# Bounds from sums of squares, a bfloat16 spread and another start of an attention and two-MLP kernel

## The chip, the core and the metric

The kernel runs on one core of a Trainium2 chip. The metric is the device time of one execution in microseconds (us); the time of a kernel is the median of its runs. The engines are TensorE (PE, with its weight loads as PEld), VectorE (DVE), ScalarE (ACT), GpSimd (POOL) and SyncE (SP), which issues the DMAs. Each engine works through its own queue in order, and waits at the head of it.

## The reference

An attention with a memory is followed by two MLPs over the same 2304 tokens:

```python
scores = where(causal, -1e9, (q @ k.T) / 8)        # B, H, S, D = 4, 8, 576, 64
a = exp(scores - max); a /= sum(a) + 1e-9
q_p = phi(q)                                       # elu(q) + 1
mem_out = (q_p @ M_prev) / (q_p . z_prev + 1e-6)
g = 1 / (1 + exp(-beta))                           # beta: one number a head
x = g * mem_out + (1 - g) * (a @ v)                # -> 2304 x 512

h = x @ w_in                                       # 512 -> 2048, first MLP
x = softplus(h) @ w_out                            # 2048 -> 512

h = x @ w2_in                                      # second MLP
P = a0 + a1*h + a2*h^2 + a3*h^3
Q = 1 + |b0|*|h| + |b1|*h^2
out = (P / (Q + 1e-6)) @ w2_out
```

The weights arrive as 8-byte floats (8 MB a matrix), and the kernel makes 4-byte floats of them by shifts and masks.

## The kernel before, in words

**Passes and blocks.** Attention goes in seven passes (`PASSES`) over parts of the four batch entries, each of two or four units of heads. Passes 0 to 2 (`FA32 = 3`) work in float32. From pass 3 on, every matrix is split into a high and a low float16 part, and a product is three float16 matmuls. After each pass the first MLP runs over its tokens in blocks (`g1`: `w_in` and softplus; `g2`: `w_out`); block 0 is in float32 (`NF32 = 1`), the others in split float16. The second MLP takes all tokens in six blocks of 384 at the end (`x2load`, `h1`, `h2_`).

**Bounds.** A split needs a power of two that keeps the numbers in float16's range, so it needs an upper bound of the operand. The kernel takes a bound for each partition, and `pmax` makes it one for all partitions: GpSimd reduces it across partitions to a number in partition 0, and a float32 matmul with a row of ones (`one`) spreads it to all 128 partitions of a PSUM bank. For the weights and for q, k and v the bound of a partition is the root of a sum of squares, from an ACT Square with its accumulator (`half_bits` halves the exponent, `ROOT` mends it). For the attention output x (`xmx`, `xgroup`), for `M_prev` (`batch_scale`) and for the second MLP's input (`x2load`) it is the largest absolute value, from a DVE `tensor_reduce`.

**What sets the order.** Nearly every instruction is recorded by one helper (so nearly all rows carry L458) and put in order by a list scheduler (`Program.order`). It walks through simulated time with its own cost for each operation, its own idea of when a DMA lands, and a key for each operation (lower goes first). An operation that may run on several engines (`flex`) goes where the model ends it sooner. For PE the scheduler looks at work only `SLACK` ns after it thinks the data is ready, as long as there is other work. The engines' queues come out of this and are fixed. Keys: `EARLY` says which inputs are loaded between the pieces of `w_in`, `KEY_W1I` and `KEY_ST` place the conversion of weight pieces, the latter that of the second MLP's, which is done during the attention (`w2_early`, tile `a`).

**Filler matmuls.** `WARM` (256 columns, tile `mask` into bank 0) and `FILL` (64 columns, `mask` into bank 7) matmuls have the lowest priority on PE and stand wherever the scheduler's model has PE idle at the start, until they are used up.

**The softplus table.** ACT has three stages of function tables (`TABLES`). The load of the second, with softplus, comes after every Exp, Ln, Abs or Sign of the first stage; `consts()` has an Exp of `beta` (tile `gg`) and an Abs of the second MLP's `b` (tile `bb`). The exponentials of the attention are softplus too.

```python
def pmax(src, n, bk=None):
    m = tn("pmx", 8, 6)[0:1, 0:n]
    G.tensor_reduce(out=m, in_=src, axis=AX.C, op=ALU.max)
    ...
    PE.matmul(out=r, lhsT=one[0:1].to_broadcast([1, 128]), rhs=m, start=True, stop=True)
```

Of the kernel before, what the change touches and what calls it, by code (L numbers as in the profile page):

```python
# [9 lines left out]
F32 = mybir.dt.float32  # L10
# [14 lines left out]
LAG = 3  # L25
SLACK = 300.0
NLOW = 1
POOL_OPS = (ALU.add, ALU.subtract, ALU.mult, ALU.max, ALU.min)

QLATE = 80  # L30
KWIN = 100.0
LMIN = 300.0
EARLY = lambda load, u, consts, batch: (
    (lambda: load(u[0], 0, 1), lambda: load(u[1], 0, 1)),
    (lambda: load(u[0], 2), batch),
    (consts,),
    (lambda: load(u[1], 2),),
)
KEY_B0 = 40
KEY_S2 = 80  # L40
KEY_W1I = 50
KEY_P = (0, 0, 0, 0)
KEY_W1O = 25
KEY_LO = -20
SL_LO = 0.5
KEY_L = -20
KEY_U2 = -30
NF32 = 1
WR0 = 6
WARM = 120  # L50
KEY_SQ = 0.0
FILL = 400
FA32 = 3
B32 = (0, 1, 2, 3, 4, 5, 6)
PEC = 2.0
# [3 lines left out]
EARLY2 = {3: (0, 16)}  # L59
KEY_ST = 160  # L60
BACKLOG = 6000.0
# [79 lines left out]
def cost(eng, name, kw):  # L141
# [5 lines left out]
    if eng == "PE":  # L147
        if name == "transpose":
            return n / 1.2 + PEC
        f32 = kw["rhs"].dtype == F32  # L150
        if n <= 8:
            return 310
        if span(out)[1] == 64:
            return 107 if f32 else 27
        return n / (0.6 if f32 else 2.4) + PEC
# [27 lines left out]
class Program:  # L183
# [151 lines left out]
    def order(self):  # L335
# [38 lines left out]
        while len(done) < len(self.ops):  # L374
# [113 lines left out]
def attn_moe_moe2(ctx, tc, q, k, v, m_prev, z_prev, beta, w1i, w1o, w2i, w2o, ca, cb, out):  # L488
# [160 lines left out]

    one = const.tile([128, 1], F32, name="one")  # L650
    off = tn("off", 1, 1)
    pcnt = [0]

    def pmax(src, n, bk=None):
        m = tn("pmx", 8, 6)[0:1, 0:n]
        G.tensor_reduce(out=m, in_=src, axis=AX.C, op=ALU.max)
        if bk is None:

            pcnt[0] += 1
            bk = bank[7][:, 320 + pcnt[0] % 24 * 8:]  # L660
# [23 lines left out]
    def consts():  # L684
        P.bulk = True
        SP.dma_start(out=gg, in_=beta.partition_broadcast(128))
        SP.dma_start(out=aa, in_=ca.partition_broadcast(128))
        SP.dma_start(out=bb, in_=cb.partition_broadcast(128))
        P.bulk = False
        A.activation(out=gg, in_=gg, func=AF.Exp, scale=-1.0)  # L690
        ts(gg, gg, 1.0, None, ALU.add)
        V.reciprocal(gg, gg)
        ts(iog, gg, -1.0, 1.0, ALU.mult, ALU.add)
        ts(iog, iog, 2.0 ** -100, None, ALU.max)
        V.reciprocal(iog, iog)
        ts(iog15, iog, 2.0 ** -15, None, ALU.mult)
        A.activation(out=bb, in_=bb, func=AF.Abs)

    def consts2():
# [12 lines left out]
        ts(fr, r, 0.5, None, ALU.mult)  # L712
# [55 lines left out]
    def batch_scale(m):  # L768
# [405 lines left out]
    def attentions32(p):  # L1174
# [8 lines left out]
        if p.i >= NF32:  # L1183
            for h in (0, 2):
                V.tensor_reduce(out=xmx[:, p.i % 3, h:h + 2], in_=p.x[:, h:h + 2], axis=AX.X, op=ALU.max, apply_absolute_value=True)

# [3 lines left out]
    def xgroup(p):  # L1190
# [4 lines left out]
        bm = tn("xm")  # L1195
        V.tensor_reduce(out=bm, in_=xmx[:, p.i % 3], axis=AX.X, op=ALU.max)
        bx, s = pow2(pmax(bm, 1), 1, "xs")
        for c in range(4):
# [133 lines left out]
    def attention(u):  # L1332
# [5 lines left out]
        if u.nh == 4:  # L1338
# [5 lines left out]
            if u.p.i >= NF32:  # L1344
                V.tensor_reduce(out=xmx[:, u.p.i % 3, h // 2:h // 2 + 2], in_=u.p.x[:, h // 2:h // 2 + 2], axis=AX.X, op=ALU.max, apply_absolute_value=True)
        else:
# [9 lines left out]
            for q0, n, c in AVC[u.i % 2][0]:  # L1356
                av_out(u, 0, q0 + 256 - u.p.q0, n, c)
            V.tensor_reduce(out=xmx[:, u.p.i % 3, h // 2:h // 2 + 1], in_=u.p.x[:, h // 2], axis=AX.X, op=ALU.max, apply_absolute_value=True)

# [96 lines left out]

    P.key = -180
    for o in RAW:
        G.memset(vw(o, (10, D), F32)[64:128], 0.0)

    P.key = -150
    w1_load(0, 0)
    P.add("POOL", "memset", lambda out: make_identity(nc, out), {"out": idf})
# [5 lines left out]
    P.pkey = 1e6  # L1469
    for _ in range(WARM):  # L1470
        PE.matmul(out=bank[0][:, 0:256], lhsT=mask[:, 0:128], rhs=mask[:, 0:256], start=True, stop=True)
    for _ in range(FILL):
        PE.matmul(out=bank[7][:, 256:320], lhsT=mask[:, 0:128], rhs=mask[:, 0:64], start=True, stop=True)
    early = EARLY(load, units, consts, lambda: batch_load(passes[0]))
    for pc in range(16):
        P.key = -149 + pc
        if pc:
            w1_load(0, pc)
        P.key += 0.5
        for step in early[pc] if pc < len(early) else ():  # L1480
            step()
        P.key = KEY_W1I + pc * 0.1
        w1_bits(0, pc)
# [8 lines left out]
    group32(passes[0])  # L1492
    P.key = -90
    batch(passes[1])
# [44 lines left out]
    for which in range(2):  # L1539
# [12 lines left out]
        if which == 0:  # L1552
# [31 lines left out]
    def x2load(j):  # L1584
# [163 lines left out]
```

## Time and profile before

| | before |
|---|---|
| median of 3 runs | 982.77 us (981.68 to 983.07) |
| the profiled execution | 979.67 us, of it 977.8 us from the first to the last instruction |
| PE, DVE, ACT, POOL busy | 946.6, 876.3, 773.9, 240.6 us |
| DMA share of the span | 51.8% of 16 engines |

The span is the time from the first to the last instruction of the profiled execution; 1.9 us of its own time lie around it. Busy times are unions of an engine's instructions. The filler matmuls count as busy PE, so PE's share of the span tells little of the first 50 us. Float32 matmuls other than transposes stand in the trace as two records each.

### The profile page before, as it was taken

To read this page: it belongs to the slowest core of one execution; us is meant where nothing else is said; L and a number is where in the kernel's file an instruction comes from. 1 tells how busy PE (TensorE), PEld (TensorE's weight loads), DVE (VectorE), ACT (ScalarE), POOL (GpSimd) and SP (SyncE) were. 2 spreads that over 40 slices of the span, in tenths; PEclk is the share of its full clock that TensorE was granted. 3 is DMA by queue.
4 is the path that set the end of the run, shared out by engine and by line. 5 is a ranking of instruction groups with operands and counts; after the bars stand their busy time and mean duration, and the time that the engine had idled before them with its cause. 6 is when DMAs were issued, how large, how long until landed. Compare 5 with 4: busy or idle time off the path is not lost. (4 is left out here: it accounts for less than half of the span.)

```text
span 977.8 us, 23547 instructions
## 1 busy us (share of the span) xinstructions
PE 946.6 (97%) x8786; PEld 693.1 (71%) x8786; DVE 876.3 (90%) x2213; ACT 773.9 (79%) x1759; POOL 240.6 (25%) x437
## 2 busy tenths in 40 slices
PE   7999999999899999899899999999999999999998
PEld 6867787878688888788799997555555555555554
DVE  4999899998988997889779979999999999989995
ACT  4997988887887886886656858878788788887885
POOL 2454342221211232122103202112304123041111
PEclk9999999999999999999999999999999999999999
DMA  9998268777999898999997420001001000000000
GB/s 235 301 260 210 66 123 172 151 137 162 166 176 182 161 166 162 173 197 254 240 299 257 162 94 2 14 1 36 32 1 65 1 34 33 1 34 1 33 1 33
DMA packets 247587, 117.94 MB, mean 121 GB/s; under 512 B 218928, under 2 KB 225072, under 8 KB 247472
## 3 DMA queue, kind: packets, MB, share of 16 engines
q1 hardware_dynamic: 247472, 116.44, 51.8%
q8 instruction: 69, 1.13, 0.5%
q14 instruction: 46, 0.38, 0.1%
HBM read 63.45 MB, written 13.63 MB: 79 GB/s over the span
## 5 line engine op out<-in xcount | busy, mean ns | idle before, releaser
L458 PE MATMUL bank<-arena,w 128*128 128x160 f16 (+3 forms) x4448 | 411.0, 251 | 4.2 <-DVE arena L458 2.8
L458 PE MATMUL bank<-arena 128*128 128x384 f16 (+9 forms) x2820 | 341.4, 293 | 13.1 <-DVE arena L458 5.9
L458 PEld LDWEIGHTS <-w 128*128 128x128 f16 x4224 | 329.7, 98 | 28.4 <-issue 8.6
L458 ACT ACTIVATE arena<-bank,tiny 128x384 f32<-128x384 f32 (+8 forms) x512 | 275.1, 585 | 44.6 <-PE bank L458 36.0
L458 PEld LDWEIGHTS <-arena 128*128 128x128 f16 (+1 forms) x2464 | 164.9, 104 | 113.6 <-issue 23.4
L458 PE MATMUL bank<-arena,gr 128*128 128x512 f16 x864 | 201.2, 379 | 0.0
L458 PEld LDWEIGHTS <-gr 128*128 128x128 f16 x864 | 84.2, 98 | 91.9
L458 POOL TENSOR_SCALAR tiny<-tiny 128x1 f32<-128x1 f32 (+6 forms) x208 | 71.3, 344 | 285.7 <-DVE tiny L458 225.4
L458 ACT ACTIVATE bank<-bank,tiny 128x512 f32<-128x512 f32 (+4 forms) x200 | 106.7, 540 | 39.6 <-PE bank L458 15.5
L458 POOL TENSOR_TENSOR arena<-arena 128x384 f32<-128x384 f32 (+5 forms) x58 | 67.2, 1160 | 231.4 <-ACT arena L458 195.8
L458 DVE SCALAR_TENSOR_TENSOR arena<-bank,tiny,arena 128x512 f16<-128x512 f32 (+5 forms) x200 | 114.0, 594 | 7.5 <-ACT arena L458 6.5
L458 ACT ACTIVATE arena<-arena,tiny 128x128 f32<-128x128 f32 (+10 forms) x164 | 98.1, 624 | 11.5 <-DVE tiny L458 5.8
L458 ACT ACTIVATE lt<-arena,qe 128x384 f32<-128x384 f32 x96 | 59.1, 615 | 33.8 <-POOL arena L458 19.8
L458 DVE SCALAR_TENSOR_TENSOR arena<-arena,tiny 128x384 f16<-128x384 f32 (+5 forms) x112 | 79.1, 729 | 4.5 <-ACT arena L458 3.3
L458 DVE CUSTOM_DVE_ANT_0 bank<-bank,mask,tiny 128x384 f32<-128x384 f32 (+4 forms) x112 | 66.8, 609 | 3.2 <-PE bank L458 2.8
L458 DVE SCALAR_TENSOR_TENSOR bank<-bank,tiny,lt 128x384 f32<-128x384 f32 x96 | 59.4, 619 | 10.9 <-ACT lt L458 10.1
L458 DVE SCALAR_TENSOR_TENSOR arena<-arena,qe,lt 128x384 f32<-128x384 f32 x96 | 66.0, 687 | 2.8 <-ACT lt L458 2.8
L458 DVE SCALAR_TENSOR_TENSOR bank<-arena,tiny,bank 128x384 f32<-128x384 f32 x96 | 59.1, 616 | 1.2
L458 ACT ACTIVATE arena<-arena 128x640 f32<-128x640 f32 (+4 forms) x75 | 46.9, 626 | 16.1 <-DVE arena L458 9.3
L458 DVE TENSOR_TENSOR arena<-arena 128x384 f32<-128x384 f32 (+5 forms) x107 | 56.7, 534 | 1.7 <-ACT arena L458 1.4
L458 DVE TENSOR_SCALAR tiny<-tiny 128x1 uint32<-128x1 uint32 (+8 forms) x306 | 49.1, 180 | 9.4 <-ACT bank L458 4.8
L458 ACT ACTIVATE gr<-arena 128x384 f16<-128x384 f32 x86 | 44.7, 520 | 10.8 <-DVE arena L458 9.6
(121 smaller groups left out, 975.0 us busy)
## 6 DMA issues: line engine op xcount, KB each, us to landing
arena<-in_moe_w_out_dram SPq DMA_DIRECT2D x32, 512.0 KB, 5.5
arena<-in_moe_w_in_dram SPq DMA_DIRECT2D x24, 512.0 KB, 5.4
arena<-in_k_dram SPq DMA_DIRECT2D x44, 128.0 KB, 3.3
arena<-in_v_dram SPq DMA_DIRECT2D x44, 128.0 KB, 3.0
arena<-arena SPq DMA_DIRECT2D x32, 160.0 KB, 2.9
arena<-x2d SPq DMA_DIRECT2D x6, 768.0 KB, 4.4
out_dram<-arena SPq DMA_DIRECT2D x18, 256.0 KB, 2.1
w<-in_moe_w_in_dram SPq DMA_DIRECT2D x8, 512.0 KB, 9.5
```

Of the source, the lines that this page charges most:

```text
L458: fn(**{k: (v.fn() if isinstance(v, Lazy) else v) for k, v in kw.items()})
```

## The change

Seven things change together. (1) `pmax` rounds its numbers to bfloat16 and spreads them by a bfloat16 matmul with `one16`. (2) The bounds of x, `M_prev` and the second MLP's input come from sums of squares (`squares`), on ACT (Square with accumulator) or DVE (`tensor_tensor_reduce`), as the scheduler likes; the products themselves, which nobody reads, go to a region of their own. Factors that follow from the bounds change with them. (3) `beta` is loaded first, then k and q of the first two units, and only then the first piece of `w_in`; the loads and the Abs of the second MLP's `a` and `b` move from `consts` to `consts2`, behind the attention. (4) The memset that clears the spare halves of the raw tiles touches 128 columns instead of 640 and comes after the masks. (5) The fillers are 800 of 64 columns; the 120 of 256 columns are gone. (6) The scheduler's model lets a DMA that queues behind others land later, and `SLACK` is 100 instead of 300. (7) Other numbers: `NLOW` 2 (two columns to an instruction that lowers the softmax bias, instead of one), `B32` (banks 4 to 6 for pass 0 instead of 0 to 6) and the keys.

```diff
-SLACK = 300.0
-NLOW = 1
+SLACK = 100.0
+NLOW = 2
...
-EARLY = lambda load, u, consts, batch: (
...
+EARLY = ("k0 q0 k1 q1", "v0 m0", "", "v1")
...
-WARM = 120
-FILL = 400
+FILL = 800
-B32 = (0, 1, 2, 3, 4, 5, 6)
+B32 = (4, 5, 6)
-KEY_ST = 160
+KEY_ST = 190
...
-                dma_free = max(dma_free, s + min(dur, 650) + 625) + o.dma
+                begin = s + min(dur, 650) + 625
+                late = max(dma_free - begin, 0.0)
+                dma_free = max(dma_free, begin) + o.dma
...
-                end = dma_free + 900
+                end = dma_free + 950 + min(0.7 * late, 1700.0)
...
-        m = tn("pmx", 8, 6)[0:1, 0:n]
+        m = tn("pmx", 4, 6).bitcast(BF16)[0:1, 0:n]
...
-        PE.matmul(out=r, lhsT=one[0:1].to_broadcast([1, 128]), rhs=m, start=True, stop=True)
+        PE.matmul(out=r, lhsT=one16[0:1].to_broadcast([1, 128]), rhs=m, start=True, stop=True)
...
     def consts():
         P.bulk = True
         SP.dma_start(out=gg, in_=beta.partition_broadcast(128))
-        SP.dma_start(out=aa, in_=ca.partition_broadcast(128))
-        SP.dma_start(out=bb, in_=cb.partition_broadcast(128))
...
+    def squares(x, acc):
...
+        P.flex(
+            (A, "activation", dict(out=out, in_=x, func=AF.Square, accum_out=acc)),
+            (V, "tensor_tensor_reduce", dict(out=out, in0=x, in1=x, scale=1.0, scalar=0.0, op0=ALU.mult, op1=ALU.add, accum_out=acc)),
+        )
...
-        V.tensor_reduce(out=mx, in_=mr, axis=AX.XY, op=ALU.max, apply_absolute_value=True)
-        _, m.s = pow2(pmax(mx, 1), 1, "ms", 2)
+        squares(mr, mx)
+        half_bits(mx)
+        _, m.s = pow2(pmax(mx, 1), 1, "ms", 2, ROOT)
...
-    P.key = -180
+    P.key = KEY_Z
     for o in RAW:
-        G.memset(vw(o, (10, D), F32)[64:128], 0.0)
+        G.memset(vw(o, (10, D), F32)[64:128, 8:10], 0.0)
+    P.key = -190
+    consts()
...
-        V.tensor_reduce(out=m, in_=x32, axis=AX.XY, op=ALU.max, apply_absolute_value=True)
-        bx, s = pow2(pmax(m, 1, bank[ab2[acnt[0] % 4 if j else 3]]), 1, "ys")
+        squares(x32, m)
+        half_bits(m)
+        bx, s = pow2(pmax(m, 1, bank[ab2[acnt[0] % 4 if j else 3]]), 1, "ys", 3, ROOT)
```

Where the scheduler puts things is seen in the queues. At the start of ACT's queue, the row after `bb` is the load of the softplus table. Before:

```order
L1323 ACT_TABLE_LOAD
L458 ACTIVATE a_99,wacc<-w_2_80 128x512
L458 ACTIVATE arena<-bank_70 128x512
L458 ACTIVATE a_99,wacc<-w_2_80 128x512
L458 ACTIVATE arena<-arena 128x512
L458 ACTIVATE arena<-bank_69 128x512
L458 ACTIVATE arena<-arena 128x512
L458 ACTIVATE arena<-bank_69 128x512
L458 ACTIVATE gg<-gg 128x8
L458 ACTIVATE bb<-bb 128x2
L208 ACT_TABLE_LOAD
L458 ACTIVATE a_99,wacc<-w_4_82 128x512
```

and of the change:

```order
L1343 ACT_TABLE_LOAD
L457 ACTIVATE gg<-gg 128x8
L205 ACT_TABLE_LOAD
L457 ACTIVATE arena<-bank_74 128x512
L457 ACTIVATE arena<-arena 128x512
L457 ACTIVATE arena<-arena,tiny 128x512
L457 ACTIVATE arena<-bank_73 128x512
```

The table load has moved from the eleventh to the third row, and waits for `beta` alone.

At the start of POOL's queue stand the six memsets of the raw tiles (`arena 64x640`), the identity and the masks, for which PE's first filler waits. Before:

```order
L471 MEMSET arena 64x640 x6
masks.py:197 MEMSET arena 128x128
masks.py:199 ISA
masks.py:199 AFFINE_SELECT arena<-arena 128x128
L471 MEMSET mask 128x384
masks.py:29 MEMSET mask 128x128
masks.py:30 AFFINE_SELECT mask<-mask 128x128
```

and of the change:

```order
masks.py:197 MEMSET arena 128x128
masks.py:199 ISA
masks.py:199 AFFINE_SELECT arena<-arena 128x128
L470 MEMSET mask 128x384
masks.py:29 MEMSET mask 128x128
masks.py:30 AFFINE_SELECT mask<-mask 128x128
L470 MEMSET arena 64x128 x6
```

The raw tiles' memsets now stand behind the masks and are a fifth as wide.

On PE in the second MLP, a bound of `x2load` stands between the products of `h2_` (`gr`) and those of the next step. Before:

```order
L458 MATMUL bank_75<-arena,gr_9554 128x512
L458 LDWEIGHTS gr_9554
L458 MATMUL bank_75<-arena,gr_9554 128x512
L458 MATMUL bank_68<-tiny,one 128x1
L458 LDWEIGHTS gr_9555
L458 MATMUL bank_69<-arena,gr_9555 128x512
```

and of the change:

```order
L457 MATMUL bank_75<-arena,gr_9877 128x512
L457 LDWEIGHTS one_114
L457 MATMUL bank_68<-tiny,one_114 128x1
L457 LDWEIGHTS arena
L457 MATMUL bank_72<-arena 128x384
```

The spread stands at the same kind of place, as one bfloat16 matmul with a weight load of its own.

## Rows read from the trace of the kernel before

**Rows 1.** The page: span, busy times by engine.

```profile
span 977.8 us, 23547 instructions
PE 946.6 (97%) x8786; PEld 693.1 (71%) x8786; DVE 876.3 (90%) x2213; ACT 773.9 (79%) x1759; POOL 240.6 (25%) x437
```

**Rows 2.** Windows: length, busy PE, PEld, DVE, ACT, POOL, clock, DMA share, GB/s.

```profile
0.00:25.00 25.00, 19.49 (x227) 17.05 (x228) 12.36 (x48) 10.89 (x29) 7.32 (x24) 1.00 0.92 238
25.00:50.00 25.00, 23.68 (x428) 19.87 (x424) 24.22 (x61) 22.60 (x68) 11.13 (x16) 1.00 1.06 296
50.00:75.00 25.00, 22.59 (x157) 15.92 (x153) 23.40 (x75) 24.94 (x79) 15.62 (x24) 1.00 1.06 258
400.00:520.00 120.00, 110.89 (x1580) 100.51 (x1579) 102.90 (x276) 81.29 (x191) 22.94 (x47) 0.99 1.06 247
650.00:950.00 300.00, 300.00 (x1620) 158.33 (x1618) 283.38 (x563) 246.47 (x486) 68.86 (x105) 1.00 0.06 22
```

**Rows 3.** Timeline of PE to 60 us: start, us, what, count, [idle before, releaser].

```profile
5.51 2.85 PE L458 MATMUL bank<-mask 128*128 128x256 bf16 x20 [5.51 <-POOL mask L471]
8.18 1.10 PE L458 MATMUL bank<-arena 128*128 128x128 f32 x4
...
14.80 13.17 PE L458 MATMUL bank<-mask 128*128 128x256 bf16 x188
...
38.53 3.96 PE L458 MATMUL bank<-mask 128*128 128x64 bf16 x130
...
48.25 0.69 PE L458 MATMUL bank<-mask 128*128 128x64 bf16 x18
...
54.40 3.62 PE L458 MATMUL bank<-arena,w 128*128 128x256 f32 x16
```

**Rows 4.** Timeline of ACT to 25 us.

```profile
19.73 0.20 ACT L458 ACTIVATE bb<-bb 128x2 f32<-128x2 f32 x1 [2.73 <-DMA bb<-in_moe_b_dram]
19.95 1.28 ACT L208 ACT_TABLE_LOAD   x1
...
21.88 0.49 ACT L458 ACTIVATE a<-a,tiny 128x256 f32<-128x256 f32 x1
```

**Rows 5.** Timeline of POOL to 20 us.

```profile
0.72 3.46 POOL L471 MEMSET arena<- 64x640 f32 x6 [0.29 <-POOLq L1732]
...
5.67 0.31 POOL masks.py:30 TENSOR_SCALAR_AFFINE_SELECT mask<-mask 128x128 bf16<-128x128 bf16 x1
...
14.48 2.62 POOL L458 TENSOR_SCALAR tiny<-tiny 128x1 f32<-128x1 f32 x8 [8.35 <-DVE tiny L458]
```

**Rows 6.** Groups of PE by form: busy us, mean ns, idle before, releasers.

```profile
L458 PE MATMUL bank<-tiny,one 1*128 1x1 f32 x38 | 7.1, 254 | 2.5 <-POOL tiny L458 2.4
L458 PE MATMUL bank<-tiny,one 1*128 1x5 f32 x32 | 6.1, 258 | 1.8 <-POOL tiny L458 1.7
```

**Rows 7.** Timeline of PE around one spread of a bound.

```profile
260.07 0.38 PE L458 MATMUL bank<-tiny,one 1*128 1x1 f32 x2
260.38 2.79 PE L458 MATMUL bank<-arena,w 128*128 128x256 f16 x24
```

**Rows 8.** Groups of DVE's reductions by form, and of ACT's Square with its accumulator.

```profile
L458 DVE TENSOR_REDUCE tiny<-arena 128x1 f32<-128x1536 f32 x6 | 10.5, 1746 | 1.8 <-DMA arena<-x2d 1.8
L458 DVE TENSOR_REDUCE xmx<-arena 128x1 f32<-128x320 f32 x12 | 5.7, 477 | 1.6 <-ACT arena L458 1.6
L458 DVE TENSOR_REDUCE xmx<-arena 128x1 f32<-128x576 f32 x4 | 3.0, 746 | 0.2 <-ACT arena L458 0.2
...
L458 ACT ACTIVATE a<-arena 128x640 f32<-128x640 f32 x18 | 13.3, 740 | 1.9 <-DMA arena<-in_v_dram 1.7
L458 ACT ACTIVATION_READ_ACCUMULATOR a<-arena 128x1 f32 x28 | 5.6, 200 | 0.0
```

**Rows 9.** Waits from 400 to 520 us: us in total, times, longest.

```profile
DVE a L458 <- DMA arena<-in_moe_w_in_dram: 11.9, 7, 4.0
...
PE bank L458 <- DVE arena L458: 4.9, 6, 2.3
```

More of the change, by code (lines that the diff above doesn't have):

```diff
@@ L25 @@
 LAG = 3
-SLACK = 300.0
-NLOW = 1
+SLACK = 100.0
+NLOW = 2
 POOL_OPS = (ALU.add, ALU.subtract, ALU.mult, ALU.max, ALU.min)
 QLATE = 80
-KWIN = 100.0
-LMIN = 300.0
-EARLY = lambda load, u, consts, batch: (
[L34 to L39, printed above, removed]
+KWIN = 30.0
+LMIN = 100.0
+EARLY = ("k0 q0 k1 q1", "v0 m0", "", "v1")
+SL_W1 = 10.0
+KEY_B1 = -90
+KEY_Z = -100
+KEY_B0 = 60
 KEY_S2 = 80
-KEY_W1I = 50
-KEY_P = (0, 0, 0, 0)
+KEY_W1I = 20
+KEY_P = (0, 0, 0, -20)
 KEY_W1O = 25
@@ L151, in cost @@
         if n <= 8:
-            return 310
+            return 310 if f32 else 64
         if span(out)[1] == 64:
@@ L650, in attn_moe_moe2 @@
     one = const.tile([128, 1], F32, name="one")
+    one16 = const.tile([128, 1], BF16, name="one16")
     off = tn("off", 1, 1)
@@ L659, in pmax @@
             pcnt[0] += 1
-            bk = bank[7][:, 320 + pcnt[0] % 24 * 8:]
+            bk = bank[7][:, 320 + pcnt[0] % 16 * 8:]
         r = bk[:, 0:n]
         pkey, P.pkey = P.pkey, -1e6
-        PE.matmul(out=r, lhsT=one[0:1].to_broadcast([1, 128]), rhs=m, start=True, stop=True)
+        PE.matmul(out=r, lhsT=one16[0:1].to_broadcast([1, 128]), rhs=m, start=True, stop=True)
         P.pkey = pkey
@@ L696, in consts, with consts2 @@
         ts(iog15, iog, 2.0 ** -15, None, ALU.mult)
+    def consts2():
+        P.bulk = True
+        SP.dma_start(out=aa, in_=ca.partition_broadcast(128))
+        SP.dma_start(out=bb, in_=cb.partition_broadcast(128))
+        P.bulk = False
         A.activation(out=bb, in_=bb, func=AF.Abs)
-    def consts2():
         A.activation(out=fa, in_=aa, func=AF.Abs)
@@ L754, in attn_moe_moe2 @@
             units.append(u)
+    jcnt = [0]
+    def squares(x, acc):
+        out = vw(RR[0] + (jcnt[0] % 3 * 320 if width(x) <= 640 else 0), (1536 if width(x) > 640 else 640,), BF16)
+        jcnt[0] += 1
+        shape = list(x.shape[1:])
+        out = out[:, 0:width(x)]
+        if len(shape) > 1:
+            names = "abc"[:len(shape)]
+            out = out.rearrange(f"p ({' '.join(names)}) -> p {' '.join(names)}", **dict(zip(names[1:], shape[1:])))
+        P.flex(
+            (A, "activation", dict(out=out, in_=x, func=AF.Square, accum_out=acc)),
+            (V, "tensor_tensor_reduce", dict(out=out, in0=x, in1=x, scale=1.0, scalar=0.0, op0=ALU.mult, op1=ALU.add, accum_out=acc)),
+        )
     def batch(m):
@@ L1184, in attentions32 @@
             for h in (0, 2):
-                V.tensor_reduce(out=xmx[:, p.i % 3, h:h + 2], in_=p.x[:, h:h + 2], axis=AX.X, op=ALU.max, apply_absolute_value=True)
+                squares(p.x[:, h:h + 2], xmx[:, p.i % 3, h // 2:h // 2 + 1])
     blk_g = []
@@ L1195, in xgroup @@
         bm = tn("xm")
-        V.tensor_reduce(out=bm, in_=xmx[:, p.i % 3], axis=AX.X, op=ALU.max)
-        bx, s = pow2(pmax(bm, 1), 1, "xs")
+        V.tensor_reduce(out=bm, in_=xmx[:, p.i % 3, 0:4 // p.units[0].nh * 2], axis=AX.X, op=ALU.add)
+        half_bits(bm)
+        bx, s = pow2(pmax(bm, 1), 1, "xs", 3, ROOT)
         for c in range(4):
@@ L1324, in attn_moe_moe2 @@
     V.memset(one, 1.0)
+    V.memset(one16, 1.0)
     V.memset(off, -OFF)
@@ L1344, in attention @@
             if u.p.i >= NF32:
-                V.tensor_reduce(out=xmx[:, u.p.i % 3, h // 2:h // 2 + 2], in_=u.p.x[:, h // 2:h // 2 + 2], axis=AX.X, op=ALU.max, apply_absolute_value=True)
+                squares(u.p.x[:, h // 2:h // 2 + 2], xmx[:, u.p.i % 3, h // 4:h // 4 + 1])
         else:
@@ L1357, in attention @@
                 av_out(u, 0, q0 + 256 - u.p.q0, n, c)
-            V.tensor_reduce(out=xmx[:, u.p.i % 3, h // 2:h // 2 + 1], in_=u.p.x[:, h // 2], axis=AX.X, op=ALU.max, apply_absolute_value=True)
+            squares(u.p.x[:, h // 2], xmx[:, u.p.i % 3, h // 2:h // 2 + 1])
     moe_next = [0]
@@ L1469, in attn_moe_moe2 @@
     P.pkey = 1e6
-    for _ in range(WARM):
-        PE.matmul(out=bank[0][:, 0:256], lhsT=mask[:, 0:128], rhs=mask[:, 0:256], start=True, stop=True)
     for _ in range(FILL):
-        PE.matmul(out=bank[7][:, 256:320], lhsT=mask[:, 0:128], rhs=mask[:, 0:64], start=True, stop=True)
-    early = EARLY(load, units, consts, lambda: batch_load(passes[0]))
+        PE.matmul(out=bank[7][:, 448:512], lhsT=mask[:, 0:128], rhs=mask[:, 0:64], start=True, stop=True).banks = set()
+    P.pkey = 0.0
+    early = {"k": lambda i: load(units[i], 0), "q": lambda i: load(units[i], 1), "v": lambda i: load(units[i], 2), "m": lambda i: batch_load(passes[i])}
     for pc in range(16):
-        P.key = -149 + pc
-        if pc:
-            w1_load(0, pc)
+        P.key = -149 + pc * SL_W1
+        for step in EARLY[pc].split() if pc < len(EARLY) else ():
+            early[step[0]](int(step[1:]))
         P.key += 0.5
-        for step in early[pc] if pc < len(early) else ():
-            step()
+        w1_load(0, pc)
         P.key = KEY_W1I + pc * 0.1
@@ L1492, in attn_moe_moe2 @@
     group32(passes[0])
-    P.key = -90
+    P.key = KEY_B1
     batch(passes[1])
```

9 lines of the change are left out of this document (4 added, 5 removed).

## The prediction

> **What bounds the kernel now.** I read the page first, then windows over the stages, then the timelines of the first 60 us engine by engine, then groups by form and waits. The page has PE busy 946.6 of 977.8 us [rows 1], but fillers are in that. The windows part the span in three. From 650 to 950 us PE is busy 300.00 of 300 us, with DVE at 283 and ACT at 246 [rows 2]: here only PE's own work counts, and what leaves its queue leaves the time. From 400 to 520, the worst stretch of the middle, PE has 110.9 of 120 us and the DMA engines are full [rows 2]. The first 50 us are another matter: PE's high share is fillers. They come as runs of one shape between short useful matmuls; the first row starts at 5.51, the last fillers at 48.25, and the first product of block 0 with weights stands at 54.40 [rows 3]. In these 50 us ACT is the late one: 10.9 of the first 25 us, then 22.6, then 24.9 of 25 [rows 2], so from about 21 us on it is what the attention of the first passes waits for. The DMA engines are full from 25 to 75 us as well [rows 2].
>
> So I price three things: work taken out of PE's queue, an earlier start, and waits in the middle.
>
> **The spread of bounds.** Each bound costs PE one float32 matmul of one or five columns, two records each: 38 and 32 records are 19 and 16 bounds, 35 in all [rows 6]. What one takes in the queue is the distance from its start to the next: 260.07 to 260.38, 0.31 us [rows 7]. In bfloat16 it is a single matmul. The trace has none of one column; the nearest row is the fillers of 64 columns, 130 in 3.96 us, 0.030 us each with their weight loads [rows 3]. The other bound is half of what it is now (one record for two), 0.155 us. I take the filler, since it too loads weights and streams few columns: 35 x (0.31 - 0.03) = 9.8 us; with the half it is 5.4. All 35 stand after the fillers, where PE is nearly always busy; in the middle, 29 of them sit behind GpSimd's reduction, for which PE waits now and then (2.4 and 1.7 us in all [rows 6]), and the change leaves that wait. I take **-9 us**.
>
> **The start.** On PE: the first filler waits 5.51 us for the mask, and POOL has the mask late because six memsets take 0.72 to 4.18 us, and ends it at 5.98 [rows 5]. Now these stand behind the masks, so PE starts near 2.5 us, 3 us earlier. The fillers: 520 of them in twelve runs take 29 us now. In the first run a pair (256 and 64 columns) takes 2.67/10 = 0.267 us, from 14.80 on 13.17/94 = 0.140 [rows 3], so the first run goes at half pace, the lower of the two clock levels (1.2 and 2.4 GHz), after an idle PE; the clock column says 1.00 for the whole stretch [rows 2]. 800 fillers of 64 columns are 800 x 0.0305 = 24.4 us at the full pace, and some 3 us more if the half pace again lasts the first 5 to 6 us: 27.5, or 1.5 less. These fillers can't be skipped, so PE alone gives 4.5 us.
>
> On ACT: the softplus table is loaded at 19.95 because the Abs of `bb` stands ahead of it and waits for its DMA until 19.73; the first exponential runs at 21.88, though its lowered bias was ready from GpSimd between 14.5 and 17.1 [rows 4, 5]. Until then ACT was idle 14 us (10.89 busy in 25 us, the last 3.75 of them after 21.25, leave 7.1 in 21.25 [rows 2, 4]). With the table loaded by about 5 us, ACT can start its saturated stretch with the first scores. Those don't come earlier by much: PE now has 120 fillers ahead of the first transposes, which at the half pace take till about 9 us, against 8.18 [rows 3]. So ACT's stretch starts 4 to 8 us earlier, not 14.
>
> Both together shorten the start by 0 if the full DMA engines or DVE (24.2 of 25 us [rows 2]) set the pace, and by 14 if ACT alone did. I take **-8 us**, a little over the middle, because all the loads of `w_in` are issued before 30 us and are used only after 54, so the DMA has room to be reordered. Banks 4 to 6 alone for pass 0 cost waits for a bank, which the fillers cover: there are 24 us of them between the useful matmuls.
>
> **The sums of squares.** DVE loses six reductions of 1.75 us, and 16 of 0.48 and 0.75 [rows 8]; with two smaller groups of four it is 24.5 us. ACT gets them as Squares: 0.74 us for 640 elements, and 0.20 for the accumulator [rows 8]. At DVE's 1.75 us for 1536 and an ACT price that grows with the elements, 0.74 x 1536/640 + 0.2 = 2.0 at most, a Square is no dearer than the reduction. DVE is the fuller engine in the middle and at the end (283 against 246 of 300 us [rows 2]), so this evens things. What hides it: PE doesn't wait for either at the end, and a bound is asked for a block ahead. Price 0, bounds -3 (DVE's waits behind it) to +5 (a Square of 2 us ahead of a PSUM evacuation on ACT, some of 30 times).
>
> The Trainium skill speaks against this move: "ScalarE: Activation LUTs", section Rules for kernel authors, sends multiplications and maxima to VectorE, not ScalarE. The rows here, in float32 and with an accumulator, have the two level, so the measurement decides; by the rule the squares would cost, and ACT with them would become the engine that is waited for, which is the third rival below.
>
> **Waits in the middle.** From 400 to 520 us DVE waits 11.9 us in seven waits for pieces of the second MLP's `w_in`, at the head of its queue, since the model thought them landed; PE waits 4.9 us for DVE there [rows 9], and PE's 9.1 idle us of 120 [rows 2] are mostly behind such. With queued transfers counted as later, the conversion stands further back. I take **-4 us**, bounds 0 and -9. The smaller `SLACK` works the other way (second rival); at 0 it is in this term's lower end.
>
> **The sum.** -9 - 8 + 0 - 4 = -21 on 977.8 gives a span of 956.8 and, with the 1.9 us around it, an execution of 958.7. The profiled execution of before (979.67) is 3.1 us under its median, so I shift by as much: 961.8, rounded to **962 us**. The own range of this case, from the terms' bounds (-5.4 - 0 + 5 - 0 and -9.8 - 14 - 3 - 9), is 947 to 982; since these ends don't fall together, 951 to 975.
>
> **Rivals.**
> *The start doesn't shrink.* DMA is at 1.06 of its engines to 75 us and DVE at 95% [rows 2]; the same bytes and the same conversions have to pass, and the first float32 passes end when they end now. Then the sum is -9 - 4 = -13, of which the fillers' 1 to 2 us may be left: 970. For it speaks that ACT's share falls to 24.9 only after DVE's rises; against it that the first 20 us have DVE and ACT half idle.
> *Slower: PE's queue blocks at its head.* With `SLACK` 100 the scheduler puts a matmul 0.1 us after it thinks its data ready, not 0.3. PE has some 700 waits for other engines in its queue; where the model is optimistic, each comes up to 0.2 us earlier against its data, and all behind it stands. Against: today's PE idles only 9.1 us in its worst 120 [rows 2], and between such waits runs of products are ready to fill. It takes 105 of these waits at the full 0.2 us to eat 21 us; at 150 of them with the start's gain gone as well, the time is 982.8 - 13 + 30 = 1000; at 150 and the rest as forecast, 992.
> *ACT becomes the bound.* If the Squares' 20 us (six of about 1.7, some twenty of 0.6) come in front of evacuations and PE waits for half of them, 10 us come back: 972. For it: ACT has to release the banks that PE fills. Against: 246 of 300 us busy [rows 2] and four banks in rotation.
> *The change to the model does nothing* to the waits for the pieces, because `KEY_ST` and the order move with it: 966, inside the forecast's range.
>
> **Chances.** The forecast 0.55 (with the last rival in it), the start's rival 0.22, ACT's 0.12, PE's head 0.11. The measurement of this kernel can't tell less than about 0.2% (2 us) from no change. Faster by over 0.2%, under 980.8: nearly all of the first three and a tenth of the last, 0.87. Within 0.2%: 0.04. Slower: 0.09. The range that leaves out no more than 2 in 10 reaches from 950 (the forecast's low end) to 978 (past the first and third rivals).
>
> **What would show it.** The rows of the spread: one bfloat16 record, the next matmul 0.03 us behind it; if it is 0.15 the first term is 5 us smaller. The first filler at 2.5 us; the second table load on ACT before 6 us; the first product of block 0 some 10 us before 54.40, and the stretch of full PE with it. In the windows of the end PE still 300 of 300. From 400 to 520 no row of DVE waiting for `w_in` by the ten, and PE over 113. The prediction is wrong if the first product comes early and PE then idles to 120 us (the start's gain given back), if PE's idle time past 150 us grows over 20 us in sum, or if ACT's rows of evacuation are what PE waits for at the end.

## The result, and the profile after

The changed kernel takes 970.5 us (median of four runs, 968.75 to 976.27) beside 982.9 us for the kernel before on the same chip: a ratio of 0.988, 95% interval 0.984 to 0.993. Measured again later it was 0.989 (0.986 to 0.993). It is faster, inside the forecast's range, but 8.5 us from the number forecast and on that of the rival whose start does not shrink.

The profiled execution, first the span and the busy row of the page (compare [rows 1]):

```profile
span 970.1 us, 24070 instructions
...
PE 941.0 (97%) x9031; PEld 688.8 (71%) x9031; DVE 861.2 (89%) x2223; ACT 792.6 (82%) x1804; POOL 227.1 (23%) x408
```

Windows of the kernel after, with the columns of [rows 2]:

```profile
25.00:50.00 25.00, 23.71 (x328) 18.62 (x325) 20.21 (x43) 19.82 (x60) 4.82 (x7) 1.00 0.99 276
50.00:75.00 25.00, 22.42 (x236) 15.75 (x234) 23.50 (x63) 22.83 (x72) 13.79 (x20) 0.86 0.92 264
75.00:100.00 25.00, 23.10 (x129) 18.30 (x128) 21.38 (x80) 23.81 (x75) 11.38 (x19) 0.93 0.66 180
400.00:520.00 120.00, 113.68 (x1670) 103.95 (x1668) 103.21 (x290) 88.01 (x211) 20.38 (x42) 1.00 1.01 240
650.00:950.00 300.00, 300.00 (x1622) 158.15 (x1621) 280.51 (x568) 250.43 (x491) 70.20 (x106) 1.00 0.06 22
```

The end is as it was: PE 300 of 300. From 400 to 520 us PE has 2.8 us more than before. New is the second row shown, 50 to 75 us: a granted clock of 0.86, and 0.93 in the third, where before had 1.00. What PE gains from 400 to 520 us it loses elsewhere. The whole stretch from 150 to 650 us, before and then after:

```profile
150.00:650.00 500.00, 483.02 (x5811) 412.08 (x5809) 447.74 (x1242) 388.99 (x902) 105.07 (x213) 0.99 0.75 162
150.00:650.00 500.00, 482.80 (x5823) 409.96 (x5821) 445.72 (x1273) 405.58 (x942) 98.84 (x202) 1.00 0.77 163
```

PE idles 17.0 us there before and 17.2 after. The span is 7.7 us shorter; 5.6 of that is less busy time of PE, and the other 2.1 less idle time, which lies in the first 150 us.

The start on PE's timeline (compare [rows 3]):

```profile
1.72 5.58 PE L457 MATMUL bank<-mask 128*128 128x64 bf16 x120 [1.72 <-POOL mask L470]
...
42.59 1.97 PE L457 MATMUL bank<-arena,w 128*128 128x256 f32 x8
...
47.72 3.72 PE L457 MATMUL bank<-arena,w 128*128 128x256 f32 x16
...
57.32 0.35 PE L457 MATMUL bank<-mask 128*128 128x64 bf16 x6
...
58.72 1.41 PE L457 MATMUL bank<-arena 64*128 64x128 f32 x10 [0.63 <-DVE tiny L457]
61.33 1.09 PE L457 MATMUL bank<-arena 128*128 128x128 f32 x4 [1.21 <-POOL tiny L457]
```

And on ACT's (compare [rows 4]):

```profile
3.58 1.28 ACT L205 ACT_TABLE_LOAD   x1
...
13.29 0.51 ACT L457 ACTIVATE a<-a,tiny 128x256 f32<-128x256 f32 x1 [1.89 <-POOL tiny L457]
```

The first filler stands at 1.72 us (before 5.51), the second table load at 3.58 (19.95), the first exponential at 13.29 (21.88), the first product with `w_in` at 42.59 (54.40). Each of these steps came, and came earlier than forecast. But the fillers are used up at 57.32, waits follow, and the clock falls. The loads of `w_in` tell why. SP's issues in the kernel before, the last two rows that load it for the first MLP:

```profile
17.88 7.57 SPq L458 DMA_DIRECT2D w<-in_moe_w_in_dram  x8
26.42 2.12 SPq L458 DMA_DIRECT2D arena<-in_moe_w_in_dram  x2
```

The same in the kernel after, from the seventh of 16 pieces on:

```profile
19.41 6.00 SPq L457 DMA_DIRECT2D w<-in_moe_w_in_dram  x5
...
32.30 1.64 SPq L457 DMA_DIRECT2D w<-in_moe_w_in_dram  x1
...
38.02 0.66 SPq L457 DMA_DIRECT2D w<-in_moe_w_in_dram  x1
...
47.36 0.42 SPq L457 DMA_DIRECT2D w<-in_moe_w_in_dram  x1
...
59.73 1.01 SPq L457 DMA_DIRECT2D arena<-in_moe_w_in_dram  x2
```

The last two pieces leave 33 us later than before, since their keys are 10 apart. What that did to the products is seen by counting them (groups by form on PE, 0 to 80 us): first before, then after.

```profile
L458 PE MATMUL bank<-arena,w 128*128 128x256 f32 x40 | 9.5, 384 | 0.0
```

```profile
L457 PE MATMUL bank<-arena,w 128*128 128x256 f32 x32 | 7.6, 385 | 0.0
```

After had all of its 32 by 52 us and not one more by 80.

### The profile page after: what moved, and what is told of

Read it like the earlier page. It is cut to its first block, busy times and chain, and to the rows that moved or that the text cites. A ratio compares the mean times of both kernels' runs of the same rounds, so it can differ in the third digit from the quotient of the medians.

```text
span 970.1 us, 24070 instructions
## 1 busy us (share of the span) xinstructions
PE 941.0 (97%) x9031; PEld 688.8 (71%) x9031; DVE 861.2 (89%) x2223; ACT 792.6 (82%) x1804; POOL 227.1 (23%) x408
## 2 busy tenths in 40 slices
DMA packets 247589, 117.97 MB, mean 122 GB/s; under 512 B 218928, under 2 KB 225072, under 8 KB 247472
## 3 DMA queue, kind: packets, MB, share of 16 engines
q1 hardware_dynamic: 247472, 116.44, 52.6%
## 4 chain that ended last, share of the span: by engine, by line
PE 54%; DVE 10%; DMA 9%; issue 3%; SPq 3%; ACT 2%; POOL 1%; DVEq 0%; POOLq 0%; ACTq 0%
PE bank L457 54%; DVE arena L457 5%; DMA arena<-arena 5%; SPq L457 3%; DVE bank L457 2%; ACT arena L457 2%; DVE tiny L457 2%; DMA arena<-in_moe_w_in_dram 2%; DMA arena<-in_moe_w_out_dram 1%; DVE a L457 1%; POOL tiny L457 1%; ACT bank L457 1%; DMA a<-arena 0%; DMA arena<-in_v_dram 0%; DMA w2d<-a 0%
## 5 line engine op out<-in xcount | busy, mean ns | idle before, releaser
L457 PE MATMUL bank<-arena 128*128 128x384 f16 (+12 forms) x2820 | 343.6, 294 | 14.8 <-DMA arena<-arena 6.5
L457 PEld LDWEIGHTS <-arena 128*128 128x128 f16 (+1 forms) x2464 | 164.9, 104 | 114.3 <-issue 22.2
L457 ACT ACTIVATE bank<-bank,tiny 128x512 f32<-128x512 f32 (+5 forms) x200 | 107.3, 542 | 40.3 <-PE bank L457 18.3
L457 POOL TENSOR_SCALAR tiny<-tiny 128x1 f32<-128x1 f32 (+5 forms) x184 | 70.1, 381 | 265.2 <-DVE tiny L457 200.5
L457 POOL TENSOR_TENSOR arena<-arena 128x384 f32<-128x384 f32 (+3 forms) x60 | 62.8, 1049 | 280.6 <-ACT arena L457 234.5
L457 DVE SCALAR_TENSOR_TENSOR arena<-bank,tiny,arena 128x384 f16<-128x384 f32 (+5 forms) x200 | 113.1, 595 | 10.2 <-ACT arena L457 9.8
L457 ACT ACTIVATE arena<-arena,tiny 128x384 f16<-128x384 f32 (+10 forms) x165 | 96.7, 616 | 13.3 <-DVE arena L457 7.7
L457 DVE SCALAR_TENSOR_TENSOR arena<-arena,tiny 128x512 f16<-128x512 f32 (+5 forms) x112 | 77.9, 718 | 7.0 <-ACT arena L457 5.1
L457 ACT ACTIVATE arena<-arena 128x512 f32<-128x512 f32 (+7 forms) x101 | 67.1, 666 | 8.1 <-DVE arena L457 3.0
L457 DVE TENSOR_SCALAR tiny<-tiny 128x1 uint32<-128x1 uint32 (+6 forms) x345 | 53.1, 170 | 5.7 <-ACT bank L457 1.3
L457 DVE SCALAR_TENSOR_TENSOR arena<-arena,bank 128x384 f32<-128x384 f32 x96 | 52.7, 549 | 0.7
```

What stands on the lines that cost most here:

```text
L457: fn(**{k: (v.fn() if isinstance(v, Lazy) else v) for k, v in kw.items()})
```

## The experiments

Ratios are to the kernel before on the same chip.

### The start alone, and where it went

The kernel before with the parts 3, 4 and 5 of the change and the first keys of part 7:

```
+EARLY = ("k0 q0 k1 q1", "v0 m0", "", "v1")
+SL_W1 = 10.0
...
-FILL = 400
+FILL = 800
-B32 = (0, 1, 2, 3, 4, 5, 6)
+B32 = (4, 5, 6)
...
+    def consts2():
+        P.bulk = True
+        SP.dma_start(out=aa, in_=ca.partition_broadcast(128))
+        SP.dma_start(out=bb, in_=cb.partition_broadcast(128))
...
-        G.memset(vw(o, (10, D), F32)[64:128], 0.0)
+        G.memset(vw(o, (10, D), F32)[64:128, 8:10], 0.0)
...
+        P.key = -149 + pc * SL_W1
```

> The kernel before with the start alone: beta, k and q loaded first, aa and bb later, the small memset behind the masks, 800 short fillers and no long ones, pass 0 in banks 4 to 6, keys of the first pieces; float32 spread, reductions, transfer model and SLACK as before. Forecast of the start: -8 us, 975 us, with useful products of TensorE ahead at 50 us and still ahead at 100 us. Theory of now (the gain is there at 50 us and gone by 80 us): 981 to 984, useful work at 100 us as before.

981.9 us, ratio 0.9996 (0.998 to 1.001). The start alone is worth nothing. Its trace has the same 32 products by 60 us and 32 by 80.

Is it the clock? More fillers keep PE busy in the hole; DVE's order doesn't change:

```
-FILL = 800
+FILL = 1000
```

> The kernel after with 1000 fillers in place of 800; DVE's order is the same, and the 200 stand between products of block 0, where the trace of after idles and falls to the half clock from 60.6 to 67.4 and from 81.1 to 84.5 us. Clock theory (the start's gain is given back because TensorE runs at half pace there): the stretches stay at the full clock, 10.2 us at half pace give back up to 5.1 us: 965 to 967 us. Supply theory (the products wait for converted pieces of w_in, whatever the clock is): the clock column goes to 1.00 and the time stays, 969 to 972. If the fillers stand ahead of work that is ready, 200 x 0.03 = 6 us are added: 976.

967.3 us, ratio 0.985 (0.982 to 0.987), where after has 0.988 and 0.989. Windows of this kernel, then of after:

```profile
60.00:70.00 10.00, 9.30 (x167) 7.57 (x167) 9.95 (x31) 9.34 (x32) 4.29 (x7) 1.00 0.99 275
70.00:80.00 10.00, 9.15 (x117) 6.68 (x114) 9.27 (x20) 9.93 (x28) 3.69 (x5) 1.00 0.88 235
80.00:90.00 10.00, 9.82 (x54) 7.72 (x52) 9.65 (x39) 9.97 (x34) 7.62 (x13) 1.00 0.78 206
```

```profile
60.00:70.00 10.00, 8.62 (x47) 5.21 (x46) 8.81 (x26) 8.55 (x29) 3.46 (x6) 0.66 0.89 279
70.00:80.00 10.00, 7.98 (x61) 5.21 (x60) 9.51 (x23) 10.00 (x30) 4.82 (x5) 1.00 0.90 239
80.00:90.00 10.00, 9.62 (x39) 7.43 (x38) 7.28 (x32) 9.13 (x31) 5.86 (x13) 0.83 0.58 145
```

The clock stays at the upper level, and yet 32 products stand at 80 us and 96 at 100, against 94 in after: the clock was not what held them. By the ratios some 4 us are gained, which is near the clock theory's number, but the intervals overlap. In another kernel with 1000 fillers (the float32 one below) the gain didn't come again; but without them that kernel's clock had fallen less (0.93 and 1.00 from 50 to 75 us in its two profiles, 0.93 from 75 to 100), so there was less to win. What the clock costs the kernel after stays open.

Is it the late pieces? The kernel after with the keys of the loads 1 apart:

```
-SL_W1 = 10.0
+SL_W1 = 1.0
```

> The kernel after with the loads of the first MLP's w_in keyed 1 apart instead of 10, so that its 16 pieces are issued one behind the other as in the kernel before (there the last by 28 us, in the trace of after at 60 us). Late-piece theory (the start's 8 us that are ahead at 50 us are given back by 80 us because block 0 waits for the last pieces): the last piece is issued before 35 us, the useful work of TensorE by 100 us is 3 to 8 us more than in the trace of after, 963 to 967 us. Conversion theory (VectorE and ScalarE have converted as much at 50 us as before, whichever order the transfers have): 968 to 973, useful work at 100 us as in after. The order behind is placed anew too, so the work by 100 us decides and not the end alone.

978.6 us, ratio 0.996 (0.994 to 0.998): by the ratios 6 to 8 us slower than after. By 80 us the trace has this many products (groups by form, 0 to 80 us):

```profile
L457 PE MATMUL bank<-arena,w 128*128 128x256 f32 x103 | 24.1, 383 | 0.2 <-ACT arena L457 0.2
```

103 in place of 32, and 155 in place of 94 by 100 us: at 0.23 us each (a run of 26 takes 5.86 us in this trace) 14 us ahead. So the late pieces were what block 0 waited for. PE is nearly full until 225 us; then comes the hole, in these windows:

```profile
200.00:225.00 25.00, 24.82 (x273) 20.57 (x271) 20.99 (x69) 20.70 (x55) 5.13 (x11) 1.00 0.91 162
225.00:250.00 25.00, 18.03 (x213) 13.21 (x211) 20.76 (x69) 19.90 (x53) 4.94 (x11) 0.92 0.89 167
250.00:275.00 25.00, 14.69 (x157) 8.35 (x157) 22.34 (x79) 16.83 (x44) 7.88 (x15) 0.64 0.91 164
```

and PE's waits from 200 to 300 us (us in total, times, the longest):

```profile
PE bank L457 <- DVE arena L457: 9.5, 7, 5.2
PE bank L457 <- DMA arena<-arena: 3.1, 5, 1.0
PE bank L457 <- ACT bank L457: 2.3, 1, 2.3
PE bank L457 <- POOL tiny L457: 2.2, 1, 2.2
```

PE idles 17 of 50 us, and the clock falls to 0.64 with it. In after the same 100 us have two such waits, 2.1 us in six for DVE and 2.6 in two for the DMA. My reading: the products of a block are also what fills PE between the steps of the attention; with them done early, PE runs dry while the attention is no further. The counts by 225 us bear that out: the float16 products of the blocks, and below them one group of the attention, first in this kernel, then in after.

```profile
L457 PE MATMUL bank<-arena,w 128*128 128x256 f16 x688 | 78.8, 273 | 0.0
L457 PE MATMUL bank<-arena 128*128 128x512 f16 x12 | 3.6, 380 | 0.0
```

```profile
L457 PE MATMUL bank<-arena,w 128*128 128x256 f16 x538 | 63.5, 273 | 1.2 <-DVE w L457 1.1
L457 PE MATMUL bank<-arena 128*128 128x512 f16 x14 | 4.2, 379 | 0.0
```

By 275 us both kernels have 768 of these products. Why the attention is no further isn't shown. With the pieces first, SP issues the next loads of k at 34.78 us, in after at 26.09, which may be part of it; and this order is placed anew, so a better one might keep the lead.

### The spread, and a place in memory

The kernel before with the bfloat16 spread, all other rows in place:

```
+    one16 = const.tile([128, 1], BF16, name="one16")
...
-        m = tn("pmx", 8, 6)[0:1, 0:n]
+        m = tn("pmx", 4, 6).bitcast(BF16)[0:1, 0:n]
...
-        PE.matmul(out=r, lhsT=one[0:1].to_broadcast([1, 128]), rhs=m, start=True, stop=True)
+        PE.matmul(out=r, lhsT=one16[0:1].to_broadcast([1, 128]), rhs=m, start=True, stop=True)
...
-    NTINY = 424
+    NTINY = 408
```

> The kernel before with the bfloat16 spread of the bounds alone; the scheduler keeps the old cost, so every other row stands where it stood. Theory (the queue pays for each bound, so what a bound gets shorter leaves the time): in the trace of after the next matmul starts 0.10 us behind a bound in the two places read so far, before it was 0.31 us; 35 x 0.2 = 7 us less, 976 us, and between 973 (0.03 us) and 977.5 (half). Rival (a bound stands behind a wait for GpSimd anyway, and the short matmul only waits longer): 0 to -2 us, 981 to 983.

978.1 us, ratio 0.996 (0.994 to 0.998): 3.8 us, between the two theories. PE's groups for the bounds, to be held against [rows 6]:

```profile
L458 PE MATMUL bank<-tiny,one 1*128 1x1 bf16 x19 | 3.2, 167 | 5.5 <-POOL tiny L458 5.0 <-ACT bank L458 0.5
L458 PE MATMUL bank<-tiny,one 1*128 1x5 bf16 x16 | 2.7, 169 | 2.6 <-POOL tiny L458 2.5
```

There are half the records, but the wait for GpSimd ahead of them went from 2.4 and 1.7 us to 5.0 and 2.5: 3.4 us more. In the trace of after the bound's price reads so:

```profile
83.47 0.18 PE L457 MATMUL bank<-tiny,one 1*128 1x1 bf16 x1
83.58 0.48 PE L457 MATMUL bank<-arena 128*128 128x128 f32 x1
```

0.11 us to the next start, against 0.31 [rows 7]. So the queue pays 35 x 0.2 = 7.0 us less, and less the 3.4 of longer waits that is 3.6, close to the 3.8 measured. The agreement is luck, though. The trace is of an execution of 982.29 us, the longest of this kernel, which has none of the gain. Against the trace of the kernel before (979.67 us) PE's busy time fell by 8.1 us (946.6 to 938.5) and its idle time grew by 10.8, and the largest part of that is not the waits ahead of bounds but PE's waits for DVE's tiles in the arena, 8.7 us before and 14.7 here. The shorter tile of small vectors moved the arena too, which matters below. What is shown is that the queue pays 7 us less and that about half of it reaches the time; that PE arrives earlier at a bound which GpSimd hasn't finished is argued.

The reverse, the kernel after with the float32 spread, should cost as much:

```
-        m = tn("pmx", 4, 6).bitcast(BF16)[0:1, 0:n]
+        m = tn("pmx", 5, 6)[0:1, 0:n]
...
-        PE.matmul(out=r, lhsT=one16[0:1].to_broadcast([1, 128]), rhs=m, start=True, stop=True)
+        PE.matmul(out=r, lhsT=one[0:1].to_broadcast([1, 128]), rhs=m, start=True, stop=True)
...
-    NTINY = 408
+    NTINY = 416
```

> The kernel after with the float32 spread put back alone, all other rows at their places. Theory (each bound costs 0.2 us of the queue): 970.5 + 7 = 977.5 us. Rival (hidden behind waits in the new order): 970.5 to 972.

965.7 us, ratio 0.983 (0.981 to 0.985): faster than after, against both theories. So after was run again, and then this kernel again, and with it the 1000 fillers:

> The kernel after once more, unchanged, on the chip of the runs beside it: 968 to 972 us, a ratio to before of 0.986 to 0.991, if the float32 spread and the 1000 fillers gained by themselves; 966 to 968 us, a ratio of 0.983 to 0.986, if the earlier difference is that of chips and executions.

971.9 us, 0.989 (0.986 to 0.993).

> The kernel after with the float32 spread once more. If the 965.7 us seen before are the kernel's (the ratio 0.983 against 0.989 of after): a ratio of 0.981 to 0.985, and again PE's idle time near 15 us. If it was the pace of the transfers in those executions (they took 49.6% of the engines' time for the bytes that take 52.6% elsewhere): 0.986 to 0.99, and idle time of 20 to 25 us. By the queue's own price, 0.2 us for each of 35 bounds, it should be 0.996.

966.9 us, 0.984 (0.981 to 0.986).

> The kernel after with the float32 spread and 1000 fillers. If both gains seen (0.6% and 0.5% below after) are real and add up: a ratio of 0.977 to 0.981, 961 to 964 us. If either was chance: 0.982 to 0.986. If both: 0.988 and more.

967.0 us, 0.985 (0.981 to 0.988). The gain of the float32 kernel came again; the fillers add nothing to it. What differs besides the spread is the last line of its edit: the tile of small vectors is longer, and the arena behind it, with all that lies behind the arena, begins elsewhere. The row of the transfer queue (packets, MB, share of the 16 engines' time) in after:

```profile
q1 hardware_dynamic: 247472, 116.44, 52.6%
```

and in the float32 kernel:

```profile
q1 hardware_dynamic: 247472, 116.44, 49.6%
```

The same packets and bytes. The next kernel is after with that line alone, its rows all in place:

```
-    NTINY = 408
+    NTINY = 416
```

> The kernel after, bfloat16 spread and all, with the tile of small vectors 8 words longer: every row of every engine stands as in after, and the arena, into which nearly all transfers go, begins 32 bytes later, at 18176 (a multiple of 64) in place of 18144 (not one). The two kernels with the float32 spread had this longer tile too, and in their profiles the same bytes took 49.6 to 50.8% of the transfer engines' time; in those with the arena at 18144 or 18208 it was 51.4 to 53.1%. Place theory (the transfers are faster by where the arena begins, and the float32 spread had nothing to do with it): the share is under 51%, and the time is the 0.984 of the float32 spread less the 0.004 that the bfloat16 spread gave alone: a ratio of 0.978 to 0.983, 961 to 966 us. Spread theory (the float32 spread itself was faster in this order): share 52.5 to 53%, ratio 0.987 to 0.991, as after.

962.0 us, ratio 0.981 (0.978 to 0.983), the fastest of all, 7 to 9 us under after by the ratios. Its queue:

```profile
q1 hardware_dynamic: 247472, 116.44, 49.6%
```

The place theory holds. With the arena where it is best, the bfloat16 spread is 0.003 faster than the float32 one (0.981 against 0.984, 3 us; the intervals overlap), in line with the 3.8 us before. This is the cleaner pair, since the arena doesn't move in it: PE's busy time is 937.4 us with the bfloat16 spread, and 943.6 and 943.0 in the two profiles with the float32 one, so here too about half of the 6 us reaches the time. But in this pair the waits for GpSimd ahead of bounds don't grow. PE's groups for the bounds in the kernel with the longer tile:

```profile
L457 PE MATMUL bank<-tiny,one 1*128 1x1 bf16 x19 | 3.1, 172 | 0.7 <-ACT arena L457 0.7
L457 PE MATMUL bank<-tiny,one 1*128 1x5 bf16 x16 | 2.8, 173 | 0.3 <-POOL tiny L457 0.3
```

That is 0.3 us of waits for GpSimd, and it is 0.4 and 0.9 in the two profiles with the float32 spread. Where the other half goes isn't shown.

### The squares

The kernel before with the sums of squares alone:

```
-            V.tensor_reduce(out=xmx[:, u.p.i % 3, h // 2:h // 2 + 1], in_=u.p.x[:, h // 2], axis=AX.X, op=ALU.max, apply_absolute_value=True)
+            squares(u.p.x[:, h // 2], xmx[:, u.p.i % 3, h // 2:h // 2 + 1])
...
-        V.tensor_reduce(out=m, in_=x32, axis=AX.XY, op=ALU.max, apply_absolute_value=True)
+        squares(x32, m)
+        half_bits(m)
```

> The kernel before with the sums of squares alone; the list schedule places everything anew by its old rules. Forecast: 0, from 979 to 985 us. Rival (what is missing of the 12 us after the spread's 4 and the start's 0 is the relief of VectorE from 150 to 520 us): 974 to 976.

983.0 us, ratio 1.000 (0.998 to 1.002): the forecast's 0.

The kernel after, the squares done by VectorE at their places:

```
-            for fn, kw in o.alts[o.eng][1]:
+            for fn, kw in o.alts["DVE" if o.idx in self.sq else o.eng][1]:
...
+        P.sq.add(o.idx)
```

> The kernel after, scheduled as it is, and each sum of squares then done by VectorE in its place in the list instead of by ScalarE: TensorE's rows and the transfers stand where they stood. Forecast (it evens two engines off the path, 0): within 3 us of the kernel after. If ScalarE's doing it carries the gain of the middle (VectorE waits and is waited for there): 5 to 10 us slower, 974 to 979.

981.1 us, ratio 0.997 (0.996 to 0.999): 9 us slower than after on the same chip (8 by the ratios). The largest squares on VectorE in this kernel, then on ScalarE in after:

```profile
L458 DVE CUSTOM_DVE_ANT_0 arena<-arena 128x1536 bf16<-128x1536 f32 x6 | 11.0, 1833 | 0.0
```

```profile
L457 ACT ACTIVATE arena<-arena 128x1536 bf16<-128x1536 f32 x6 | 8.9, 1478 | 1.2 <-DMA arena<-x2d 1.1
```

PE's waits from 150 to 520 us, here:

```profile
PE bank L458 <- DVE arena L458: 8.4, 14, 1.6
...
PE bank L458 <- DVE tiny L458: 1.8, 1, 1.8
```

In after these two are 4.4 us in ten and 0.4 in one. So in after's order ScalarE's squares are worth 9 us, and in before's order nothing. The two aren't the same test: the kernel before was placed anew for the squares, while here they were pushed onto VectorE in lists laid out for ScalarE, and no run places after's order anew with VectorE's squares. That a removed load pays where the order puts something in its place is a reading that fits, not one that is shown.

### The transfer model

The kernel before with queued transfers counted and `SLACK` 100:

```
+                late = max(dma_free - begin, 0.0)
-                end = dma_free + 900
+                end = dma_free + 950 + min(0.7 * late, 1700.0)
-SLACK = 300.0
+SLACK = 100.0
```

> The kernel before with queued transfers counted and SLACK 100 alone. Forecast: -4 us, 978, with VectorE's 11.9 us of waits for w_in from 400 to 520 us nearly gone. Rival 1 (what is missing of the 12 us is the model's): 973 to 975. Rival 2 (KEY_ST sets when the pieces are converted, the model does nothing): 981 to 984. The slower rival of the prediction (TensorE's queue blocks at its head): over 990, with TensorE's waits grown all along.

977.8 us, ratio 0.995 (0.993 to 0.997): 4.9 us. DVE's waits for `w_in` from 400 to 520 us, 11.9 us in [rows 9], are

```profile
DVE a L460 <- DMA arena<-in_moe_w_in_dram: 5.1, 5, 2.1
```

and the window has PE at 113.49 us of 120 (110.9 before). In the kernel after the same wait is back:

```profile
DVE a L457 <- DMA arena<-in_moe_w_in_dram: 11.2, 6, 5.7
```

with PE at 113.68 all the same. So what PE has in that window doesn't hang on that wait. It also isn't steady: in the second profile of after PE has 111.74 there. And it isn't where the 4.9 us lie: from 150 to 650 us PE idles 16.0 us in this kernel and 17.0 before, and the execution in this trace, of 980.14 us, is 2.3 us above the kernel's median. The size of the gain is measured, its place isn't found, and `SLACK` and the change to the model weren't run apart.

## Why the prediction was right or wrong

**Direction and range** were right, but 17 of the 21 us forecast lay in two terms of which one came to nothing and the other to less than half. That the time fell within the range is owed to the range's width, and to 2 to 3 us that no term names.

**The start, -8 us, failed.** Alone it measured 0 (0.9996). The step that failed is "all the loads of `w_in` are issued before 30 us and are used only after 54, so the DMA has room to be reordered". The change used that room: its keys put the last pieces at 59.73 us, and block 0 stood at 32 products until 80 us. The prediction named this outcome ("the first product comes early and PE then idles") without seeing it in the order of SP's queue, where it could have been read: the last piece stands behind the loads of later units. The half clock in this stretch, which the prediction didn't expect, comes on top, but isn't what held the products. The start's rival had the right number, 970, by luck, since 9 of its 13 us were a spread that gave 3.8; it had half the reason: the DMA engines are full, but the pieces were late because others went first. (Its row is read the wrong way round: ACT's busy time rises to 24.9 us of 25, it doesn't fall.) With the pieces early the lead was there (103 products by 80 us), and was given back from 225 to 275 us.

**The spread, -9 us, was 3.8.** Two parts were off. The row behind the bound is 0.11 us after it, not 0.03, so the filler was the wrong neighbour and the half (0.155) the nearer one: 7 us. And the sum has no term for idle time that grows elsewhere, which took about half: 3.8 us are left alone, and 3 in the pair with the arena in one place. That "the change leaves that wait" failed in the first of these (the wait for GpSimd grew by 3.4 us) and held in the second.

**The middle, -4 us, measured -4.9 alone.** The size was right, the mechanism isn't borne out: DVE's wait fell to 5.1 us in that kernel and is back at 11.2 in after, and PE's idle time from 150 to 650 us is 17.0 us before, 16.0 in that kernel and 17.2 in after. The sign "no row of DVE waiting for `w_in` by the ten" failed, and "PE over 113" came without it.

**The squares, 0, measured 0 alone** (1.000), with the order free to move. The rule weighed in the prediction, of the Trainium skill's "ScalarE: Activation LUTs", section Rules for kernel authors, which sends multiplications and maxima to VectorE, doesn't hold for these, in float32 and with an accumulator: 1.48 us (and 0.20 for the accumulator) on ScalarE, 1.83 on VectorE, and 9 us slower with the squares moved there. So the term's 0 is right for before's order and not shown for after's. ACT did not become the bound: at the end PE is busy 300 of 300 us.

**The slower rival** (PE's queue blocks at its head with `SLACK` 100) didn't come: the kernel with the model and `SLACK` alone was faster.

**The sum** of the parts alone is 3.8 + 4.9 + 0 + 0 = 8.7 us, the whole 10.4 to 11.5. The other 2 to 3 us lie with the remaining keys, `NLOW` or how the parts act together; that wasn't taken apart. The diff also hides a gain that wasn't taken: `NTINY` moves the arena from one place at which the transfers take longer to another (18208 to 18144), and a third (18176) gives 7 to 9 us more.

## What to carry to other kernels

A stage that starts earlier gains only if its last input comes earlier too: look for the last piece in the queue that loads it, not the first, and then ask which later stage lived on the work that is now done. What an instruction costs in its queue is a bound of what shortening it gives: here about half of it came back as idle time. Look whether the trace that you read is of an execution that has the gain, before you add up its waits. And after any change to the size of a small tile look at where the big one behind it begins, since here a shift of 32 bytes was worth 7 to 9 us where the whole change brought 10 to 11.5.

## What the runs showed of the hardware that was not expected

**The place of the arena.** Where it begins at 18176 bytes (71 x 256), the 247,472 packets took 49.6 to 50.8% of the engines' time in four profiles. In the four with the layout of the kernel before (18208, 32 further on) it was 51.5 to 52.0%, in the six at 18144 (32 less) 51.4 to 53.1%. After and its padded twin are the same in every row and differ by 0.8% of the time for it. Nine tenths of what the transfers take longer is in the 208,384 packets of 256 bytes: a mean of 23.8 ns in after and 21.6 in the twin, while the 15,488 packets of 2048 bytes took 97.8 and 98.0. How this reaches the end of the kernel wasn't followed. The Trainium skill's "DMA: Bandwidth & Descriptors", section How a descriptor splits into AXI transactions, says of reads that one which doesn't start at a multiple of 256 bytes begins at the boundary below and fetches bytes that nobody uses. The runs agree in the direction only. Most loads write into the arena and don't read it, and the slots of the arena begin at multiples of 256 from its start, so by that section's way of counting, as an estimate, a packet of 256 bytes read from there would cost 9 beats (of 32 bytes) at 18208 and 15 at 18144 in place of 8; measured, the two places hardly differ (23.4 to 23.5 ns, and 23.1 to 24.5, against 21.4 to 22.2). Both are 32 past a multiple of 64, which fits 64 better than 256 as the multiple that counts; no run has the arena at a multiple of 64 that isn't one of 256.

**The clock.** In after it stood at the lower level, 1.2 GHz, for a part of the windows from 60 and 80 us (0.66 and 0.83 on average): the first after waits of 0.63 and 1.21 us, the second after one of 1.48 at 78.59 us. With fillers in those places it stayed at the upper one, and the products by 100 us differ by two.
